# Linear attention and two MLPs: chunks 0 to 3 in 128-token tiles, the last eight chunks spread over two job slots each

## The chip, the cores and the metric

One core of a Trainium2 chip runs the whole program. The metric is device microseconds per execution; lower is better. TensorE is called PE here, its weight loads PEld, VectorE DVE, ScalarE ACT, and the queue of SyncE, from which nearly all DMAs are issued, SP.

## The reference

Attention with a decaying state (4 batches, 8 heads, 768 tokens, 64 features), then two MLPs over 3072 tokens (512 to 2048 to 512), the first gated by h times sigmoid(1.702 h), the second with a slope per feature for negative values:

```python
for t in range(S):
    state = gamma[None, :, None, None] * state + np.einsum('bhd,bhe->bhde', k[:, :, t], v[:, :, t])
    y[:, :, t] = scale * np.einsum('bhd,bhde->bhe', q[:, :, t], state)
x = np.ascontiguousarray(attn_out.transpose(0, 2, 1, 3)).reshape(B * S, H * D)
h = x @ w_in;  g = h * (1.0 / (1.0 + np.exp(-1.702 * h)));  x = g @ w_out
h = x @ w_in2; g = np.maximum(h, 0.0) + alpha * np.minimum(h, 0.0); out = g @ w_out2
```

The weights of both MLPs come in 64-bit floats.

## The kernel before

**Chunks.** The tokens are cut into 24 chunks of 128, six to a batch. A chunk needs two loads of 512 KB, qk (queries and keys by feature) and kv (keys and values by token). `att_v` (L326) scales the values by the decay on ACT, eight ops. `att_products` (L334) makes the products of a chunk in two halves of 64 tokens, each for four pairs of heads and two heads of a pair: scores `sc` (key times query), updates `pu` (key times value), and the output `px`, once from the state (`mid` in a chunk's middle, `diag` at its start) and once from the chunk's own scores `a`. That is 4 x 16 products of 64 by 64 by 64 in 32-bit floats; the trace records each as two matmuls with a weight load each. In one `att_step` (L381) the output of chunk `o` alternates with scores and updates of chunk `new`. After them DVE masks the scores (`a`, L400), adds up the state (`mid` L414, `diag` L418 and L419) and scales the output (`att_x`, L421): for chunks 0 to 7 into `x` (L427), which ACT rounds to `xhi` (L431) and DVE completes with `xlo` (L455), for later chunks into four pieces of `xl` (L446).

**The MLPs.** A block is 512 tokens. Blocks 0 and 1 (chunks 0 to 7) run through the first MLP in plain form: 32 steps, each one `mlp_h` (L538, 12 matmuls of 512 columns, `ph`) and one `mlp_y` (L554, 12 matmuls, `py`). Five steps are of block 0, 16 of block 1, and 11 of block 0 again. All the rest (`h_unit` L635, `y_chunk` L703) uses Strassen's scheme on pairs of blocks: 7 products in place of 8, in units of 6 matmuls (`pa`, `pd`) on prepared sums of inputs (`xo`, L472 and L473) and of weights (`hw`, `yw`, loaded in pieces of 256 KB). The first Strassen product is of chunks 8 to 15, the second of chunks 16 to 23.

**Order.** `job(slot, fn, ...)` books work in job slots. Slots below 0 are the launch, slots 0 to 63 lie two to a plain step (base = 64), and from 64 on there is a slot every 3.5 units. Within a slot `rank` sorts. Program order gives priorities, `tc.high_priority` raises the attention's DVE work, and a scheduler fixes each engine's order when the kernel is built. The PSUM banks are h (2), a (2) and y0 to y3; `py` holds y0 to y3 through the whole plain part.

**Chunks in slots.** Chunks 0 to 3 run in slots -10 to -2, chunks 4 to 7 in 0 to 8, chunks 8 to 15 in 36 to 52, always two slots apart, and chunks 16 to 23 in 64 to 72, one slot apart. The first `ph` of block 0 needs xhi of chunk 3, that of block 1 xhi of chunk 7. An output step of one chunk is also the scores' step of the next.

**Loads.** A ring of five 512 KB tiles (`issue`, L141) takes weights and most chunks in the order of use; a place comes free with `done`. Chunks in LOADS and chunks 1 to 3 go instead into four of the 82 SBUF slots each (`load_early`, L161). SP issues all of them in order. Weights are converted from 64-bit floats on ACT and DVE (L181 to L218), stored and loaded again as pieces; the Strassen sums of weights (L260, L283) are booked in slots 37 to 69, the Strassen inputs in 53 to 62.

**Constants.** The mask and the decays stand in `cst`; its first 76 columns are loaded first (L875).

```python
turn_at.setdefault(s, {})["new"] = c
turn_at.setdefault(s + gap, {})["o"] = c
attention(c, s - 3 if c < per else s - 1, s + gap)
```

Of the kernel before, what the change touches and what calls it, by code (L numbers as in the profile page):

```python
# [14 lines left out]
AF = mybir.ActivationFunctionType  # L15
# [4 lines left out]
P = 128  # L20
# [8 lines left out]
NLEAD = HC + H + NP  # L29
# [11 lines left out]
NQ = NF // 2  # L41
X_OF = ("b11", "b21", "t2", "t1", "t3", "b22", "t4")
# [17 lines left out]
LOADS = {5: -1, 6: 1, 7: 3}  # L60
LOADS.update({16 + n: s for n, s in enumerate((-5, -3, -1, 1, 2, 3, 4, 5))})
# [8 lines left out]
def tile_linear_attention_two_mlps(ctx: ExitStack, tc, qk, kv, w1, w2, consts, alpha, out):  # L70
# [22 lines left out]
    causal = cst[:, 0:HC]  # L93
    decay_v = cst[:, HC:HC + H]
    decay_c = cst[:, HC + H:NLEAD]
# [65 lines left out]
    def load_early(c):  # L161
        early[c] = []
        for key in (("qk", c), ("kv", c)):
            ts = []
            for n in range(2):
                ts.append(take("early"))
                nc.sync.dma_start(out=ts[n], in_=src_of(key)[:, n * 512:(n + 1) * 512])
            early[c] += ts
            loaded[key] = ts
# [154 lines left out]
    last_v = {}  # L324

    def att_v(c):  # L326
        v = take("v", (P, 2 * NP, D))
        vt = loaded["kv", c][1].rearrange("p (n d) -> p n d", d=D)
        for n in range(2 * NP):
            last = nc.scalar.activation(out=v[:, n, :], in_=vt[:, n, :], func=AF.Copy, scale=decay_v[:, n:n + 1])  # L330
        last_v[c] = last.ins
        att["v", c] = v
# [47 lines left out]

    def att_step(o, new):  # L381
        if o is not None:
            att["px", o] = att_psum(o, "px")
        if new is not None:
            att["sc", new] = att_psum(new, "sc")
            att["pu", new] = att_psum(new, "pu")
        att_products(o, new)
        if o is not None:
            give(att.pop(("v", o)), att.pop(("a", o)), att.pop(("mid", o)))
            loaded.pop(("qk", o))  # L390
            loaded.pop(("kv", o))
            if o in early:
                give(*early.pop(o))
            else:
                done()
                done()
        with tc.high_priority(HG):
            if new is not None:
                a = att["a", new] = take("a", (P, 2 * NP, HC))
                nc.vector.tensor_tensor(  # L400
                    out=a, in0=att.pop(("sc", new)).rearrange("p (n i) -> p n i", i=HC),
                    in1=causal.unsqueeze(1).to_broadcast([P, 2 * NP, HC]), op=ALU.mult,
                )
                att_state(new)
            if o is not None:
                att_x(o)
# [14 lines left out]
    def att_x(c):  # L421
        if c >= 2 * BT // C:
            att_x_kept(c)
            return
        x32 = take("x32", (P, NP, C))
        px = att.pop(("px", c)).rearrange("p (n i) -> p n i", n=NP)
        nc.vector.tensor_tensor(out=x32, in0=px, in1=decay_out, op=ALU.mult)  # L427
        j, i = divmod(c, BT // C)
        if i == 0:
            new_x(j)  # L430
        hi = nc.scalar.copy(out=x_hi[j][:, :, i * C:(i + 1) * C], in_=x32)  # L431
        if c < BT // C:
            tc.add_manual_dep(
                hi.ins, last_v[min(c + 2, BT // C - 1)].name,
                mybir.DependencyInfo(mybir.DependencyClass.NoSync, mybir.DependencyReason.DATA), reason="behind v",
            )
        att["x", c] = x32

    def att_x_kept(c):
        px = att.pop(("px", c)).rearrange("p (n i) -> p n i", n=NP)  # L440
        t, i = divmod(c % (2 * BT // C), BT // C)
        for k in range(2):
            for d in range(2):
                if i == 0:
                    xl[k, d, t] = take("xl")
                nc.vector.tensor_tensor(  # L446
                    out=xl[k, d, t][:, i * C:(i + 1) * C], in0=px[:, 2 * d + k, :],
                    in1=decay_out[:, 2 * d + k, :], op=ALU.mult,
                )
# [25 lines left out]
    def x_load(idx, t):  # L475
        assert ("x", idx) in stored
        for k in range(2):
            for d in range(2):
                xl[k, d, t] = take("xl")
                nc.sync.dma_start(out=xl[k, d, t], in_=xsd[idx][k, :, d, t])  # L480

    def x_prep(idx, n):
        which = X_OF[n]
        for k in range(2):
            sub = lambda o, x, y: nc.vector.tensor_tensor(out=o, in0=x, in1=y, op=ALU.subtract)
            if which == "t2":
                t1, t2 = xt[idx, "t1", k], xt[idx, "t2", k] = take("t1"), take("t2")
                sub(t1, xl[k, 0, 1], xl[k, 0, 0])
                sub(t2, xl[k, 1, 1], t1)
                give(xl.pop((k, 0, 0)))  # L490
            if which == "t3":
                xt[idx, "t3", k] = take("t3")
                sub(xt[idx, "t3", k], xl[k, 1, 1], xl[k, 0, 1])
                give(xl.pop((k, 0, 1)))
            if which == "t4":
                xt[idx, "t4", k] = t = xt.pop((idx, "t2", k))
                sub(t, xl[k, 1, 0], t)
                give(xl.pop((k, 1, 0)))
            if which[0] == "b":
                x_split(idx, n, k, xl[k, int(which[1]) - 1, int(which[2]) - 1])  # L500
                if which == "b22":
                    give(xl.pop((k, 1, 1)))
# [287 lines left out]
    def attention(c, s_v, s_out):  # L790
        if c in LOADS:
            job(LOADS[c] + (base if c >= 4 * per else 0), load_early, c)
            job(s_v, att_v, c)
        else:
            job(s_v, att_v, c, load=(("qk", c), ("kv", c)))
        if c < 2 * per:
            job(s_out + 1, att_x_low, c)

# [11 lines left out]
    turn_at = {}  # L810
# [54 lines left out]
    rank = [conv_hi, att_x_low, att_step, att_v]  # L865
# [92 lines left out]
def _consts():  # L958
# [4 lines left out]
    causal = np.tile(i[None, :HC] >= i[:HC, None], (2, 1))  # L963
# [3 lines left out]
    decay_v = gamma[head][:, None, :] ** -at[:, :, None]  # L967
    decay_c = gamma[head] ** C
    parts = [causal, decay_v.reshape(P, H), decay_c, decay_out.reshape(P, NP * C)]
# [44 lines left out]
```

## Time and profile before

| | |
|---|---|
| median of 3 runs | 1047.96 us (1047.56 to 1048.35) |
| the profiled execution | 1051.6 us, its span 1049.6 us |
| PE busy | 1022.6 us (97%) |
| DVE busy | 871.1 us (83%) |
| ACT busy | 679.9 us (65%) |
| DMA | 289.49 MB, mean 276 GB/s |
| chain that ended last | PE 93%, ACT 3%, DMA 1%, issue 1%, DVE 1% |
| instruction queue (q8) | 56 packets, 0.92 MB |

The span runs from the first to the last instruction. A busy PE is not PE at its peak: matmuls overlap, and their ends are modelled, so rates are better read from start to start. "issue" is time in which an engine waited for nothing that the profile shows.

### The profile page before, as it was taken

Reading aid. Unit: us, or ns where it says so; the run is one execution under the profiler, and the core shown is the slowest. Engines: PE = TensorE matmul, PEld = TensorE weight load, DVE = VectorE, ACT = ScalarE, POOL = GpSimd, SP = SyncE. Lnnn points to the kernel's source line nnn. Section 1 sums busy time; section 2 is a strip of 40 time slices with the busy share of each in tenths; the row PEclk is TensorE's granted clock in tenths of the full one; section 3 lists DMA queues with packets and bytes.
Section 4 is the critical chain, followed back from the end, with each engine's and each line's share of the span. In section 5 each row is a group of like instructions: output and inputs, shape, how many; then the busy total and the mean of one; then the engine's idle time right before and its main releaser. Section 6 shows DMA issues by size and latency. Waiting matters only on the chain.

```text
span 1049.6 us, 20177 instructions
## 1 busy us (share of the span) xinstructions
PE 1022.6 (97%) x7084; PEld 842.0 (80%) x7084; DVE 871.1 (83%) x1730; ACT 679.9 (65%) x1408; POOL 0.2 (0%) x4
## 2 busy tenths in 40 slices
PE   7889999999989999999999999999999999999998
PEld 5768888788768888888888888888888888888886
DVE  4899836898769999979799999998686987678792
ACT  5787744656766786665687686785555865556740
POOL 0000000000000000000000000000000000000000
PEclk8799999999989999999999999999999999999999
DMA  9669937899999799979989899986686676675661
GB/s 351 217 190 346 393 102 249 292 320 330 376 366 397 244 325 356 341 277 345 341 291 351 295 322 356 309 283 218 220 272 220 219 231 174 224 256 172 199 201 60
DMA packets 146405, 289.49 MB, mean 276 GB/s; under 512 B 16512, under 2 KB 16768, under 8 KB 146304
## 3 DMA queue, kind: packets, MB, share of 16 engines
q1 hardware_dynamic: 146016, 288.04, 80.1%
q8 instruction: 56, 0.92, 0.4%
q14 instruction: 45, 0.37, 0.1%
q10 hardware_dynamic: 288, 0.17, 0.1%
HBM read 213.69 MB, written 74.45 MB: 275 GB/s over the span
## 4 chain that ended last, share of the span: by engine, by line
PE 93%; ACT 3%; DMA 1%; issue 1%; DVE 1%; SPq 0%; DVEq 0%
PE py L720 36%; PE pa L647 21%; PE pd L647 16%; PE ph L545 7%; PE py L564 7%; PE px L341 3%; PE sc L341 1%; PE pu L341 1%; ACT cvr L183 1%; DMA wo<-wo 1%; ACT cvt L181 1%; PE idle L889 1%; DMA ld<-kv 0%; ACT wb L214 0%; ACT v L330 0%
## 5 line engine op out<-in xcount | busy, mean ns | idle before, releaser
L720 PE MATMUL py<-gh,yw 128*128 128x512 f32 x1120 | 299.7, 389 | 0.0
L720 PEld LDWEIGHTS py<-gh,yw 128*128 128x128 f32 x1120 | 210.2, 188 | 43.7
L647 PE MATMUL pa<-xo,hw 128*128 128x512 f32 x912 | 232.1, 391 | 0.4 <-ACT gw L516 0.4
L647 PEld LDWEIGHTS pa<-xo,hw 128*128 128x128 f32 x912 | 171.5, 188 | 37.3 <-ACT v L330 0.9
L529 DVE TENSOR_TENSOR gl<-gw,gh 128x512 fp32r<-128x512 f32 x240 | 161.4, 690 | 38.3 <-ACT gh L528 33.7
L528 ACT CAST gh<-gw 128x512 fp32r<-128x512 f32 x240 | 145.6, 620 | 56.2 <-PE py L720 26.9
L647 PE MATMUL pd<-xo,hw 128*128 128x512 f32 x684 | 176.0, 393 | 2.0 <-DVE s L260 2.0
L720 PE MATMUL py<-gl,yw 128*128 128x512 f32 x560 | 172.8, 389 | 0.0
L647 PEld LDWEIGHTS pd<-xo,hw 128*128 128x128 f32 x684 | 129.2, 189 | 29.5 <-DVE s L260 2.4
L720 PEld LDWEIGHTS py<-gl,yw 128*128 128x128 f32 x560 | 105.0, 188 | 22.1 <-DVE gl L529 0.4
L734 DVE TENSOR_TENSOR yc<-py,yc 128x512 f32<-128x512 f32 x99 | 63.8, 687 | 27.5 <-PE py L720 27.5
L521 DVE SCALAR_TENSOR_TENSOR gw<-t,nalpha,gw 128x512 f32<-128x512 f32 x96 | 71.6, 749 | 14.8 <-ACT gw L520 14.6
L519 ACT ACTIVATE t<-gw 128x512 f32<-128x512 f32 x72 | 45.5, 632 | 55.0 <-DVE gw L662 52.0
L545 PE MATMUL ph<-xhi,wb 128*128 128x512 f32 x256 | 67.4, 407 | 5.7 <-ACT xhi L431 5.5
L214 ACT CAST wb<-s 128x256 fp32r<-128x256 f32 x128 | 47.7, 402 | 31.2 <-DVE s L260 19.9
L659 ACT COPY gw<-pa 128x512 f32<-128x512 f32 x80 | 46.7, 584 | 29.5 <-PE pa L647 27.5
L564 PE MATMUL py<-gh,wb 128*128 128x512 f32 x256 | 65.4, 398 | 0.0
L545 PEld LDWEIGHTS ph<-xhi,wb 128*128 128x128 f32 x256 | 49.9, 196 | 17.3 <-ACT xhi L431 6.1
L662 DVE TENSOR_TENSOR gw<-pd,gw 128x512 f32<-128x512 f32 x80 | 55.1, 688 | 3.7 <-PE pd L647 2.9
L218 DVE TENSOR_TENSOR wb<-s,wb 128x256 fp32r<-128x256 f32 x128 | 49.8, 423 | 9.8 <-ACT wb L214 9.5
L564 PEld LDWEIGHTS py<-gh,wb 128*128 128x128 f32 x256 | 47.5, 189 | 10.5
L683 DVE TENSOR_TENSOR gw<-gw 128x512 f32<-128x512 f32 x80 | 53.9, 691 | 0.4
(90 smaller groups left out, 1366.6 us busy)
## 6 DMA issues: line engine op xcount, KB each, us to landing
hw<-wcin SPq DMA_DIRECT2D x266, 256.0 KB, 5.0
yw<-wcout SPq DMA_DIRECT2D x232, 256.0 KB, 3.8
ld<-w SPq DMA_DIRECT2D x64, 512.0 KB, 5.8
wcin<-wb SPq DMA_DIRECT2D x112, 256.0 KB, 5.1
wcout<-wb SPq DMA_DIRECT2D x88, 256.0 KB, 5.0
yw<-wo SPq DMA_DIRECT2D x48, 256.0 KB, 5.3
wo<-wb SPq DMA_DIRECT2D x32, 256.0 KB, 6.2
early<-qk SPq DMA_DIRECT2D x28, 256.0 KB, 5.8
```

What stands on the lines that cost most here:

```text
L218: nc.vector.tensor_tensor(out=w[:, 256:], in0=src, in1=w[:, 0:256].bitcast(F32), op=ALU.subtract)
L341: nc.tensor.matmul(out=ps[rows[half], cols], lhsT=lhsT, rhs=rhs, start=begin, stop=True, skip_group_check=True,)
L521: nc.vector.scalar_tensor_tensor(out=g, in0=t, scalar=nalpha[:, ft:ft + 1], in1=g, op0=ALU.mult, op1=ALU.add)
L528: nc.scalar.copy(out=gh, in_=g)
L529: nc.vector.tensor_tensor(out=gl, in0=g, in1=gh.bitcast(F32), op=ALU.subtract)
L545: nc.tensor.matmul(out=ph, lhsT=cols(w, low, k), rhs=x[:, k, :], start=(n == 0), stop=(n == len(prods) - 1),)
L564: nc.tensor.matmul(out=py[e], lhsT=lhsT, rhs=g, start=(begin and seen[e] == 1), stop=(end and seen[e] == 3))
L647: nc.tensor.matmul(out=ps, lhsT=w[:, 256 * part_ + k * P:256 * part_ + (k + 1) * P], rhs=x[2 * k + low], start=(n in (0, 1, 3) and m == 0) ...
L662: nc.vector.tensor_tensor(out=g, in0=ps, in1=g, op=ALU.add)
L683: sub = lambda o, x, y: nc.vector.tensor_tensor(out=o, in0=x, in1=y, op=ALU.subtract)
L720: nc.tensor.matmul(out=ps[e], lhsT=w[:, at:at + P], rhs=t, start=(fresh and seen[e] == 1), stop=(m == GQ - 1 and seen[e] == 3), skip_group ...
L734: add_ = lambda o, x: nc.vector.tensor_tensor(out=o, in0=ps, in1=x, op=ALU.add)
```

## The change

Chunks 0 to 3 are no longer cut into halves of 64 tokens. `launch_scores` makes their scores with all 128 keys of a pair's head against all 128 queries, into two banks, and masks them with two DVE ops; `launch_out` makes updates over 128 tokens, the output from the state and from the chunk, the new state without `mid`, and the output's scaling. Each chunk has PSUM banks of its own (`AT_LAUNCH`), and the steps of neighbouring chunks are no longer interleaved. Mask, decays and the layout of kv come in a second form for them.

Chunks 16 to 23 get a step every two slots from slot 56 on: four of them lie in the plain part (56 to 62), four in the Strassen part (64 to 70), with the last output in slot 72 as before. PSUM banks follow the slot. All chunks but 0 to 3 and 8 to 13 are loaded into SBUF slots, five job slots ahead (14 and 15 four); kv is let go after the chunk's own step, qk one step later. The tiles of `xl` are kept apart by product.

```diff
-NLEAD = HC + H + NP
+NLEAD = C + HC + 2 * H + NP
+NLAUNCH = BT // C
-LOADS = {5: -1, 6: 1, 7: 3}
-LOADS.update({16 + n: s for n, s in enumerate((-5, -3, -1, 1, 2, 3, 4, 5))})
+ATT2 = (-8, 2)
+RINGED = (8, 9, 10, 11, 12, 13)
+LEADS = ((), (5, 1), (5, 1), (4, 1), (5, 1), (5, 1))
...
+    AT_LAUNCH = (
+        {},
+        {"sc0": "y0", "sc1": "y1", "pu": "y2", "px": "y3"},
+        {"sc0": "h", "sc1": "h", "pu": "y0", "px": "y1"},
+        {"sc0": "y2", "sc1": "y3", "pu": "h", "px": "h"},
+    )
+
     def att_psum(c, which):
-        if c < BT // C:
-            tag = {"sc": "h", "pu": f"y{c % 2}", "px": f"y{2 + c % 2}"}[which]
-        elif c < 4 * BT // C:
+        if c < NLAUNCH:
+            tag = AT_LAUNCH[c].get(which, "a")
+        elif which == "sc" and turn_of[c] < base or which != "sc" and turn_of[c] + 2 < base:
             tag = {"sc": "h", "pu": "a", "px": "a"}[which]
...
+    def launch_scores(c):
+        qt, kt = loaded["qk", c]
+        att_v(c)
+        ps = [att_psum(c, f"sc{s}").rearrange("p (n i) -> p n i", n=NP) for s in range(2)]
+        for p in range(NP):
+            at = slice(p * C, (p + 1) * C)
+            for s in range(2):
+                nc.tensor.matmul(
+                    out=ps[s][:, p, :], lhsT=kt[ROWS[s], at], rhs=qt[ROWS[s], at], start=True, stop=True,
+                )
+        a = att["a", c] = []
+        for s in range(2):
+            a.append(take(f"a{s}", (P, NP, C)))
+            with tc.high_priority(HG):
+                nc.vector.tensor_tensor(
+                    out=a[s], in0=ps[s], in1=causal[C].unsqueeze(1).to_broadcast([P, NP, C]), op=ALU.mult
+                )
+
+    def launch_out(c):
...
+        for p, s, _, h in heads:
+            product(pu, s, slice(p * D, (p + 1) * D), kt[:, h * D:(h + 1) * D], v[:, h, :])
+        if c:
+            for p, s, at, h in heads:
+                product(px, 1 - s, at, diag[c % 2][ROWS[s], p, :], qt[ROWS[s], at])
+        for p, s, at, h in heads:
+            product(px, 1 - s, at, v[:, h, :], a[s][:, p, :])
...
+            if c:
+                nc.vector.tensor_tensor(out=new, in0=src, in1=diag[c % 2], op=ALU.add)
+                src = new
+            dec = decay_c.unsqueeze(2).to_broadcast([P, NP, D])
+            nc.vector.tensor_tensor(out=new, in0=src, in1=dec, op=ALU.mult)
+            att_x(c)
...
-            loaded.pop(("qk", o))
-            loaded.pop(("kv", o))
-            if o in early:
-                give(*early.pop(o))
-            else:
-                done()
-                done()
+            leave("qk", o)
+        if new is not None:
+            leave("kv", new)
...
-        hi = nc.scalar.copy(out=x_hi[j][:, :, i * C:(i + 1) * C], in_=x32)
-        if c < BT // C:
-            tc.add_manual_dep(
...
+        nc.scalar.copy(out=x_hi[j][:, :, i * C:(i + 1) * C], in_=x32)
...
     for c in range(NCH):
-        if c < per:
-            s, gap = 2 * c - 2 * per - 2, 2
-        elif c < 2 * per:
+        if c < NLAUNCH:
+            s = 2 * c - 2 * per - 1
+            job(s, launch_scores, c, load=(("qk", c), ("kv", c)))
+            job(s + 1, launch_out, c)
+            job(s + 2, att_x_low, c)
+            continue
+        if c < 2 * per:
             s, gap = 2 * (c - per), 2
+            job(s + gap + 1, att_x_low, c)
         elif c < 4 * per:
             s, gap = ATT1 + 2 * (c - 2 * per), 2
         else:
-            s, gap = base + c - 4 * per, 1
+            s, gap = base + ATT2[0] + ATT2[1] * (c - 4 * per), ATT2[1]
+        turn_of[c] = s
         turn_at.setdefault(s, {})["new"] = c
         turn_at.setdefault(s + gap, {})["o"] = c
-        attention(c, s - 3 if c < per else s - 1, s + gap)
+        if c in RINGED:
+            job(s - LEADS[c // per][1], att_v, c, load=(("qk", c), ("kv", c)))
+        else:
+            job(s - LEADS[c // per][0], load_early, c)
+            job(s - LEADS[c // per][1], att_v, c)
```

## Rows read from the trace of the kernel before

**Rows 1.** The page's head.
```profile
span 1049.6 us, 20177 instructions
```

**Rows 2.** Busy time by stage: stretch, length, busy us (x instructions) per engine, granted clock, DMA.
```profile
6.45:31.35 24.90, 15.67 (x497) 14.77 (x496) 15.12 (x33) 15.09 (x48) 0.00 (x0) 0.78 0.89 334
...
47.40:75.70 28.30, 23.67 (x378) 18.89 (x376) 27.28 (x66) 25.93 (x61) 0.00 (x0) 0.99 0.69 217
...
152.00:219.00 67.00, 65.61 (x1188) 54.36 (x1187) 51.87 (x144) 36.37 (x105) 0.00 (x0) 1.00 0.76 253
219.00:251.30 32.30, 32.30 (x145) 26.70 (x144) 30.67 (x74) 20.86 (x53) 0.00 (x0) 1.00 0.99 359
251.30:279.00 27.70, 27.70 (x499) 23.03 (x499) 21.34 (x56) 16.27 (x44) 0.00 (x0) 1.00 0.97 340
...
330.60:1049.60 719.00, 715.28 (x3155) 591.68 (x3153) 612.94 (x1085) 465.91 (x867) 0.00 (x0) 1.00 0.79 265
```

**Rows 3.** PE's waits, whole span: for whom, us in total, times, longest.
```profile
PE px L341 <- issue: 11.5, 4, 3.7
PE ph L545 <- ACT xhi L431: 5.5, 2, 4.1
...
PE pu L341 <- ACT v L330: 1.4, 1, 1.4
```

**Rows 4.** Timeline of ACT in the launch: start, us, op, [idle before <-releaser].
```profile
14.67 2.02 ACT L330 ACTIVATE v<-early,cst 128x64 f32<-128x64 f32 x8 [2.34 <-DMA early<-kv]
...
18.91 2.02 ACT L330 ACTIVATE v<-early,cst 128x64 f32<-128x64 f32 x8
...
30.68 0.62 ACT L431 CAST xhi<-x 128x512 fp32r<-128x512 f32 x1 [3.17 <-DVE x L427]
```

**Rows 5.** The launch by stretches that end at PE's stops, columns as in rows 2.
```profile
0.00:12.40 12.40, 11.19 (x221) 7.32 (x222) 4.03 (x10) 7.05 (x21) 0.20 (x4) 1.00 0.86 314
12.40:17.90 5.50, 2.99 (x128) 2.73 (x126) 3.03 (x7) 3.23 (x11) 0.00 (x0) 1.00 1.05 394
17.90:26.10 8.20, 4.66 (x126) 4.49 (x127) 5.17 (x14) 4.54 (x14) 0.00 (x0) 0.65 1.00 383
```

**Rows 6.** Timeline of PE where block 1 begins.
```profile
70.55 1.08 PE L564 MATMUL py<-gl,wb 128*128 128x512 f32 x4
75.68 3.78 PE L545 MATMUL ph<-xhi,wb 128*128 128x512 f32 x8 [4.05 <-ACT xhi L431]
...
84.10 1.98 PE L545 MATMUL ph<-xhi,wb 128*128 128x512 f32 x8
```

**Rows 7.** Stretches of small products alone and in full step, and block 1's first step.
```profile
36.77:39.06 2.29, 2.29 (x65) 2.23 (x64) 0.81 (x2) 2.18 (x6) 0.00 (x0) 0.86 0.98 354
...
159.88:161.90 2.02, 2.02 (x129) 1.95 (x129) 0.64 (x2) 1.32 (x3) 0.00 (x0) 1.00 0.00 0
...
75.70:82.00 6.30, 6.30 (x15) 4.95 (x16) 4.97 (x13) 2.43 (x5) 0.00 (x0) 0.52 0.99 259
```

**Rows 8.** DVE's groups in 251.3 to 309: count, busy us, mean ns, idle before.
```profile
L446 DVE TENSOR_TENSOR xl<-px,cst 128x128 f32<-128x128 f32 x20 | 5.2, 284 | 3.6 <-PE px L341 3.6
...
L400 DVE TENSOR_TENSOR a<-sc,cst 128x512 f32<-128x512 f32 x6 | 4.1, 686 | 3.5 <-PE sc L341 3.5
...
L414 DVE TENSOR_TENSOR mid<-pu,diag 128x256 f32<-128x256 f32 x5 | 2.1, 417 | 0.0
```

**Rows 9.** Line 647 (Strassen units) in 279.6 to 308.9: PE, PEld, clock, DMA.
```profile
279.60:308.90 29.30, 17.43 (x60) 13.02 (x61) 0.83 1.02 372
```

**Rows 10.** Chunk loads issued in 251 to 345: KB each, median us to landing.
```profile
early<-kv SPq DMA_DIRECT2D x12, 256.0 KB, 5.4
early<-qk SPq DMA_DIRECT2D x10, 256.0 KB, 5.4
```

**Rows 11.** Timeline of PE around a change to small products.
```profile
157.06 1.98 PE L545 MATMUL ph<-xhi,wb 128*128 128x512 f32 x8
158.88 1.07 PE L545 MATMUL ph<-xlo,wb 128*128 128x512 f32 x4
159.88 0.27 PE L341 MATMUL px<-ld,diag 64*64 64x64 f32 x2
```

More of the change, by code (lines that the diff above doesn't have):

```diff
@@ L92, in tile_linear_attention_two_mlps @@
     cst = cpool.tile([P, NCONST], F32, name="cst")
-    causal = cst[:, 0:HC]
-    decay_v = cst[:, HC:HC + H]
-    decay_c = cst[:, HC + H:NLEAD]
+    causal = {n: cst[:, at:at + n] for n, at in ((C, 0), (HC, C))}
+    decay_v = {n: cst[:, at:at + H] for n, at in ((C, C + HC), (HC, C + HC + H))}
+    decay_c = cst[:, C + HC + 2 * H:NLEAD]
     decay_out = cst[:, NLEAD:].rearrange("p (n i) -> p n i", n=NP)
@@ L161, in load_early @@
     def load_early(c):
-        early[c] = []
+        early[c] = {}
         for key in (("qk", c), ("kv", c)):
@@ L322, in att_psum @@
         return pool_.tile([P, 512], F32, tag=tag, name=which)
-    last_v = {}
+    ROWS = [slice(s * D, (s + 1) * D) for s in range(2)]
+    def launch_scores(c):
[15 more added lines that the diff above has]
+                )
@@ new lines, in launch_out, with product @@
+    def launch_out(c):
+        v, a = att.pop(("v", c)), att.pop(("a", c))
+        qt = loaded.pop(("qk", c))[0]
+        kt = loaded.pop(("kv", c))[0]
+        px, pu = att_psum(c, "px"), att_psum(c, "pu")
+        fresh = set()
+        def product(ps, half, cols, lhsT, rhs):
+            begin = (id(ps), half) not in fresh
+            fresh.add((id(ps), half))
+            nc.tensor.matmul(
+                out=ps[ROWS[half], cols], lhsT=lhsT, rhs=rhs, start=begin, stop=True, skip_group_check=True,
+            )
+        heads = [(p, s, slice(p * C, (p + 1) * C), 2 * p + s) for p in range(NP) for s in range(2)]
+        for p, s, _, h in heads:
[5 more added lines that the diff above has]
+            product(px, 1 - s, at, v[:, h, :], a[s][:, p, :])
+        give(v, *a)
+        if c in early:
+            give(*early[c]["qk"], *early[c]["kv"])
+        else:
+            done()
+            done()
+        att["px", c] = px
+        with tc.high_priority(HG):
+            src, new = pu[:, :NP * D].rearrange("p (n d) -> p n d", n=NP), diag[(c + 1) % 2]
+            if c:
[4 more added lines that the diff above has]
+            att_x(c)
@@ L326, in att_v @@
     def att_v(c):
         v = take("v", (P, 2 * NP, D))
+        dec = decay_v[C if c < NLAUNCH else HC]
         vt = loaded["kv", c][1].rearrange("p (n d) -> p n d", d=D)
         for n in range(2 * NP):
-            last = nc.scalar.activation(out=v[:, n, :], in_=vt[:, n, :], func=AF.Copy, scale=decay_v[:, n:n + 1])
-        last_v[c] = last.ins
+            nc.scalar.activation(out=v[:, n, :], in_=vt[:, n, :], func=AF.Copy, scale=dec[:, n:n + 1])
         att["v", c] = v
@@ L379, in att_products, with leave @@
                 f(*args, s)
+    def leave(kind, c):
+        loaded.pop((kind, c))
+        if c in early:
+            give(*early[c][kind])
+        else:
+            done()
     def att_step(o, new):
@@ L478, in x_load @@
             for d in range(2):
-                xl[k, d, t] = take("xl")
-                nc.sync.dma_start(out=xl[k, d, t], in_=xsd[idx][k, :, d, t])
+                xl[idx, k, d, t] = take("xl")
+                nc.sync.dma_start(out=xl[idx, k, d, t], in_=xsd[idx][k, :, d, t])
     def x_prep(idx, n):
@@ L788, in job @@
         jobs.setdefault(int(slot), []).append((fn, args, load))
[L790 to L797, printed above, removed]
     def convert(key, slot):
@@ L982, in by_token @@
     def by_token(a):
-        a = a.reshape(B, NP, 2, CPB, 2, HC, D).transpose(0, 3, 2, 5, 4, 1, 6)
-        return a.reshape(NCH, P, H * D)
+        whole = a.reshape(B, H, CPB, C, D).transpose(0, 2, 3, 1, 4).reshape(NCH, P, H * D)
+        a = a.reshape(B, NP, 2, CPB, 2, HC, D).transpose(0, 3, 2, 5, 4, 1, 6).reshape(NCH, P, H * D)
+        return np.concatenate([whole[:NLAUNCH], a[NLAUNCH:]])
     def weights(w_in, w_out, swap):
```

43 lines of the change are left out of this document (22 added, 21 removed).

## The prediction

> **What bounds the kernel now.** I read the page's head first [rows 1]: a span of 1049.6 us, and 1051.6 us for that execution, so 2.0 us lie around the span. The median of the runs is 1047.96 us, 3.6 below the profiled execution; I take every difference from the trace and set it off against the median. Next came the table of stages [rows 2]. The reader is to see that TensorE (PE) is the bound nearly everywhere (715 of 719 us from 330.6 on), that it is idle in three places alone, 6.45 to 31.35 (15.7 of 24.9 busy), 47.4 to 75.7 (23.7 of 28.3) and after 279, and that DVE and the DMA engines are almost full in 219 to 251.3 (30.7 of 32.3; 0.99). What follows a stage that has been shortened is therefore PE work that moves up whole. The list of PE's waits [rows 3] names them: 11.5 us for nothing that the profile shows, all at small products, and 5.5 us for xhi.
>
> **Launch: what the stops are.** Cut at PE's three stops, the launch shows 221 + 222 instructions of PE and its weight loads up to 12.4, then 128 + 126, then 126 + 127 [rows 5]: a stop every 250 or so, while DMA is at 0.86 to 1.05. The page's instruction queue brought 56 packets of 0.92 MB in all, 16 KB each. I read the stops as waits for the next piece of program, behind full DMA engines. That the cause is code is my inference; the counts are rows.
>
> **Launch: the sum.** Before, a chunk has 64 small products, each two records with a weight load each: 256 instructions. After, it has 8 scores, 8 updates, 8 from the state (none for chunk 0) and 8 from the chunk: 128. Up to chunk 3's last product that is 24 (warm) + 480 = 504 instructions against 1016, so one stop in place of three, and it falls within chunk 3, where PE waits for data anyway. What then sets the end is data: chunk 2's v waits for its DMA until 14.67, chunk 3's v begins at 18.91 and takes 2.02 [rows 4], and the loads of chunks 0 to 3 keep their order. So v ends at 20.9. Behind it come the last updates and 16 records of 128 columns. Their form is not in the trace; bounds are the 64-column stream beside nothing else, 64 records in 2.29 us or 36 ns each (0.6 us), and double that (1.2), and I add one more for the updates and take 1.7. Then x (0.69, the shape of a [rows 8]) and xhi 0.62 [rows 4], with hand-overs 1.4. The first ph comes at 20.9 + 1.7 + 1.4 = 24.0 instead of 31.35: **-7.3 us**. Bounds: 22.5 (-8.9), if products trail v closely; 29 (-2.4), if two stops of 2.5 fall behind v.
>
> Before, all launch products have one shape, 64 by 64; now K and M change three to four times a chunk. The row for a change of shape: four ph<-xlo records ahead of small products take 1.00 us (158.88 to 159.88), eight before them 1.82 or 0.23 each [rows 11], so 0.09 us for the change. Four changes on chunk 3 are 0.4 us, inside the 1.7. The Trainium skill ("TensorEngine Tiling (Array Packing)", Key Properties) says that a change of tiling mode drains the engine, which speaks against this part. By that rule all 16 changes would cost; at the row's price that is 1.4 us, with 0.4 of it behind the last data, so the sum stays; no row shows a change between two small shapes.
>
> DVE gets a second a (0.69) and loses mid (0.42) per chunk [rows 8], +1.1 us in all, on an idle engine. The first piece of constants grows from 39 to 109 KB, 0.2 us at 394 GB/s [rows 5], ahead of a v that waits for kv: nothing. Chunk 4 leaves the ring, chunks 5 to 7 load two slots earlier: each puts 1 MB, 2.7 us, ahead of weights on SP's queue, but the weights get the ring's two places; 0 to 2.7, I take 0 here, as the next term holds it.
>
> **Ramp (to 75.68).** The first ph of block 1 waits until 75.68 for chunk 7's xhi, 4.05 us after PE ran dry [rows 6]. From 47.4 DVE has 27.3 of 28.3 us busy [rows 2]. By 31.35 it had done 15.1 us of the launch stage's 24.9; done at the same share by 24.0, it is 7.3 x 0.61 = 4.5 us behind, plus 1.1: 0 to 5.6 us of the gain is lost where DVE binds. PE's steps there are near to back to back, so I lean to the low end: **+1.5 us**.
>
> **Four chunks moved in front of the Strassen part.** PE: a chunk's 128 records take 2.02 us between large products [rows 7], the same before and after the move. DVE: a 0.69, mid and the two diag 0.42 each, xl 4 x 0.28 [rows 8], 3.1 us a chunk, 12.4 for four; in 219 to 251.3 it has 1.6 us free, so some 10 us of sums and splits slide past 251.3, where 6.4 are free [rows 2] and the moved chunks' own 12.4 are gone. Cover: the sums are wanted units later. Uncovered: up to 9.2 us at the first units. SP and DMA: 16 issues of 256 KB, 10.6 us, go into stages with shares of 0.76 and 0.99. ACT: 4 x 2.0 of v, with a third free. Chunk 19's updates take y2, so they wait for the last py; behind them on PE stand the products of chunks 19 and 20 and the first Strassen units, and who waits is DVE for mid: one lone burst, 0.3 us (64 records alone 2.29, beside others 128 in 2.02 [rows 7]). The chunk tiles now sit in SBUF slots while weights still fill most of the 82; a load that waits for its slot holds SP, with stores of sums and the hw loads queued behind it. No row shows a full SBUF; 0 to 4.1 us, PE's longest wait for another engine [rows 3]; I take 0.4, as nine earlier chunks cost little. Against that the nearest row: nine such bursts in 152 to 219 cost PE one wait of 1.4 us, for v [rows 3]. I take **+1.5 us**, bounds 0.5 to 9.2.
>
> **Strassen start.** In 279.6 to 308.9 the 60 large records [rows 9] need 60 x 0.227 = 13.6 us, two whole bursts 4.0, changes 0.9: 18.5 of 29.3. So 10.8 us are lost: PE stands still, and after it a part runs at the lower of its two levels, 1.2 of 2.4 GHz (granted 0.83 as a mean). DMA is at 1.02, and each load stands in one line with the hw pieces that PE's next units need. Of that stage's loads 12 + 10 are chunk loads of 256 KB [rows 10]; six or so remain. Half the bursts, at twice the distance, 10 us of DMA less. I take 60% of the loss: **-6.5 us**, bounds -2 and -10.8.
>
> Sum: -7.3 + 1.5 + 1.5 - 6.5 = -10.8, so 1047.96 - 10.8 = **1037.2 us**.
>
> **Rivals.**
> (1) DVE eats the launch's gain in the ramp, all 5.6, and 1.7 more as weights come late: the launch nets 0, total -5.0, 1043. For: DVE's 27.3 of 28.3. Against: PE too is nearly full from 47.4 until the stop.
> (2) Slower: DVE's excess before 251.3 stands in front of PE. 9.2 lost there; the launch nets -1.7 by the same engine; the Strassen start gains 4 of 10.8, since what slides comes to lie there: +3.5, 1051.5. It decides from the point where PE waits for DVE in all over 10 us in the ramp and around 251.3. For: 1.6 us free. Against: PE waits for DVE before 251.3 hardly at all [rows 3], so its order leaves room.
> (3) Stops come with full DMA, not with the count of instructions: two stops remain behind v (-2.4), bursts stop as now (-2), the plain part pays 1.5: -2.9, 1045. For: every stop lies at a share near 1.0. Against: 250 instructions each time.
> (4) The dry 4.05 us ahead of 75.68 goes too, and with it the slow clock behind it: 0.52 granted in 75.7 to 82 [rows 7], so nearly all at 1.2 of 2.4 GHz, after PE had stood still. The step begun at 75.68 ends at 84.10, 8.42 us for 24 records that take 5.45 at 0.227 [rows 6]: 3.0 lost. -7.1 more: 1030. For: chunk 7's small products lie ahead of the py at 70.55, so PE was done with them five us before xhi; against: the priorities that order DVE's work stay.
> (5) The change doesn't do what it says: the launch ends later than its data, for the 128-column products run at a quarter of the stream's rate or ACT's v queue behind conversions (ph at 29, -2.4), and the moved chunks cost in front what they free behind: 1045.5 to 1049, no change that can be told.
>
> **How the numbers follow.** Forecast (1032 to 1041) 0.44; (1) 0.17; (2) 0.12; (3) 0.10; (4) 0.12; (5) 0.05. The range takes in (4) with a deeper Strassen gain, 1026, and ends below (2), 1047. A measurement of this kernel tells 0.2%, 2.1 us, from no change. Faster: 0.44 + 0.17 + 0.10 + 0.12 = 0.83; same 0.05; slower 0.12.
>
> **What would show it.** Launch: one stop of PE, none of the three in place; first ph near 24; the scores of chunk 3 done before its v. Ramp: first ph of block 1 near 70. Plain end: no wait of PE for DVE between 200 and 251 on the new clock, small products of chunk 19 just behind the last y. Strassen: the 30 us from the first hw unit hold some 22 us where they held 29. Wrong if ph starts past 28, if block 1's first ph hasn't moved by 4 us, or if pa or pd wait at the first units for xo or for wb.

## The result, and the profile after

| | kernel before | changed kernel |
|---|---|---|
| median, 6 runs each | 1048.1 us (1046.4 to 1051.4) | 1053.9 us (1052.6 to 1058.8) |
| ratio, 95% interval | 1 | 1.0061 (1.0036 to 1.0087) |
| profiled execution, its span | 1051.6, 1049.6 us | 1056.6, 1054.8 us |

The change makes the kernel 5.8 us slower where I forecast 10.8 us faster; my range ended at 1047. Since the gain of the launch is there, some 13 us or more were lost elsewhere. One table finds the place. I matched TensorE's large matmuls of the two traces, each kind by its order, and compared their start times:

```
matmul (us in the kernel before)        after     difference
first ph                31.35           26.86      -4.5
block 1's first ph      75.68           70.98      -4.7
a py at                195.2           188.3       -6.8
a py at                210.8           210.7       -0.2
a ph at                213.7           215.9       +2.3
first pd               254.0           272.7      +18.7   (8.4 of it: four chunks' products, moved)
a pd at                330.6           334.6       +4.0
last py               1045.5          1050.6       +5.2
```

The reader is to see three things. Launch and ramp did about what I forecast. From 195.2 to 254.0 TensorE falls back by 25.5 us; a chunk's products take some 2.1 us there [rows 7], so 8.4 us is work that was moved and **17 us is lost**, 9.1 of it by 213.7, ahead of the first moved chunk. And from there to 330.6 it gains 14.7, 6.3 beyond the 8.4.

The page's head of the changed kernel, and stages that answer to [rows 2] (columns as there):

```profile
span 1054.8 us, 19672 instructions
```
```profile
6.28:26.86 20.58, 16.50 (x231) 12.45 (x227) 15.55 (x33) 15.88 (x47) 0.00 (x0) 1.00 1.05 394
42.90:70.98 28.08, 23.25 (x378) 18.92 (x376) 26.96 (x65) 25.38 (x59) 0.00 (x0) 0.97 0.58 167
147.20:219.00 71.80, 65.42 (x1126) 53.32 (x1124) 47.78 (x131) 35.45 (x106) 0.00 (x0) 0.95 0.87 309
219.00:272.70 53.70, 49.67 (x636) 40.68 (x633) 48.22 (x123) 31.77 (x92) 0.00 (x0) 0.97 0.82 274
```

Before, TensorE was busy throughout from 219 to 279 and had 1.4 us idle from 152 to 219 [rows 2]; now it has 6.4 us idle up to 219 and 4.0 behind it, and part of both stretches runs at a lower granted clock. DVE is not what is full: 48.2 of 53.7. What TensorE waits for (against [rows 3]):

```profile
PE ph L609 <- ACT xhi L499: 5.9, 2, 4.1
PE pa L711 <- ACT gw L580: 4.5, 2, 3.5
PE px L406 <- issue: 4.1, 1, 4.1
PE px L406 <- DVE diag L486: 3.5, 3, 1.9
PE py L628 <- ACT gh L592: 1.8, 1, 1.8
...
PE pu L406 <- DVE y L642: 0.9, 1, 0.9
```

The three stops of the launch are gone; one stop "issue" of 4.1 us is new, at 206 us, and behind it the clock falls to its lower level (0.51 granted, nearly all at 1.2 of 2.4 GHz, TensorE having stood idle):

```profile
210.00:216.00 6.00, 5.74 (x19) 4.49 (x19) 3.96 (x13) 2.61 (x10) 0.00 (x0) 0.51 1.02 344
```

Just ahead of it TensorE waits 1.9 us for diag (202.2 to 204.1), and ahead of that VectorE waits, in order, for a store (until 181.5 us). VectorE's waits from 150 to 200 us, changed kernel, then the kernel before:

```profile
DVE s L262 <- DMA wcin<-wb: 5.6, 1, 5.6
```
```profile
DVE s L260 <- DMA wcin<-wb: 0.3, 1, 0.3
```

A sum tile (s) wants an SBUF slot whose last tenant (a wb) has not been written out yet. That suggests a shortage of slots. It can be counted from the code: the fewest free ones of the 82 that any take finds, by job slot.

```
job slot       42  43  44  45  46  47  48  50  52  54  56  57  58  59  60  61  62  63
before          4   5  16  15  13  11  15  21  28  34  32  29  35  29  30  29  28  24
after           4   5  12  11   5   3   9  19  24  26  19  11  18  11  17  15  19  15
```

At 44 to 49 the difference is chunks 14 and 15, which left the ring of loads (RINGED ends at 13); from 51 on it is chunks 16 to 19. The sum that waits is booked in job slot 45. There it finds 12 free slots where it found 16, and since chunk 14's four tiles have just taken the oldest, it gets the slot of a weight piece made in job slot 42, in the kernel before of one made in 38. The lowest count alone is no sign of such a wait: both kernels come down to 4 at job slot 42 and to 3 at 76, and the kernel before waits for no store at either place.

### The profile page after: what moved, and what is told of

The parts are those of the page before. It is cut to its first block, busy times and chain, and to the rows that moved or that the text cites. A ratio compares the mean times of both kernels' runs of the same rounds, so it can differ in the third digit from the quotient of the medians.

```text
span 1054.8 us, 19672 instructions
## 1 busy us (share of the span) xinstructions
PE 1025.5 (97%) x6828; PEld 841.5 (80%) x6828; DVE 870.5 (83%) x1730; ACT 675.7 (64%) x1407; POOL 0.2 (0%) x4
## 4 chain that ended last, share of the span: by engine, by line
PE 69%; DVE 14%; DMA 9%; ACT 6%; issue 2%; SPq 1%; DVEq 0%; ACTq 0%
PE py L784 30%; PE pa L711 16%; PE pd L711 11%; PE ph L609 5%; PE py L628 5%; DVE gl L593 2%; DMA wcout<-wb 2%; DVE wb L220 2%; DVE s L262 1%; DMA ld<-kv 1%; ACT v L396 1%; DVE gw L585 1%; DVE gw L726 1%; DMA wcin<-wb 1%; DMA wo<-wo 1%
## 5 line engine op out<-in xcount | busy, mean ns | idle before, releaser
L711 PE MATMUL pd<-xo,hw 128*128 128x512 f32 x684 | 173.1, 389 | 0.0
L216 ACT CAST wb<-s 128x256 fp32r<-128x256 f32 x128 | 48.2, 402 | 39.1 <-DVE s L262 25.6
L628 PE MATMUL py<-gh,wb 128*128 128x512 f32 x256 | 68.8, 413 | 1.8 <-ACT gh L592 1.8
L185 ACT ACTIVATE cvr<-ld 128x512 uint16<-128x512 uint32 x64 | 50.5, 789 | 5.5 <-DVE wsum L285 2.9
```

The source lines that it names most:

```text
L185: nc.scalar.activation(out=low, in_=w0.bitcast(U32), func=AF.Copy, scale=2.0**-29)
L216: nc.scalar.copy(out=w[:, 0:256], in_=src)
L628: nc.tensor.matmul(out=py[e], lhsT=lhsT, rhs=g, start=(begin and seen[e] == 1), stop=(end and seen[e] == 3))
L711: nc.tensor.matmul(out=ps, lhsT=w[:, 256 * part_ + k * P:256 * part_ + (k + 1) * P], rhs=x[2 * k + low], start=(n in (0, 1, 3) and m == 0) ...
```

## Theories, and the experiments

**Slots**: loads that sit in slots four or five job slots ahead make slots scarce; VectorE and SyncE's queue then wait in order for stores and releases. **VectorE**: the moved chunks' 12.4 us, or simply a full VectorE behind 195 us, take whatever TensorE gained. **Code blocks**: the "issue" stop is TensorE waiting for its program, and where it falls is a matter of position. All ratios below are to the kernel before, run on the same chip; 1 in 1000 is 1.05 us. One kernel's runs differ by some us (the kernel before: 1041.8 to 1051.4 in all), so sizes are read from the ratios, places from the traces. The difference of two ratios is uncertain by 2 to 3 us, their two intervals taken together.

### Which loads, and which place

e1_ring1415, e2_ring1619 and e3_ring1419 send chunks through the ring again (for e2: 16 to 19; for e3: 14 to 19):

```diff
-RINGED = (8, 9, 10, 11, 12, 13)
+RINGED = (8, 9, 10, 11, 12, 13, 14, 15)
```

> Chunks 14 and 15 are loaded through the ring of loads again, as before the change; the other changed chunk loads stay in job slots. Slot theory: in the changed kernel the early tiles of chunks 14 and 15 hold 8 of the 82 SBUF slots, a weight sum then waits 5.6 us on VectorE for a store to leave its slot (at 176 us), and from this come the TensorE waits between 200 and 216 us (9.1 us lost there). It expects that this wait goes, that TensorE has no gap over 1 us from 195 to 216 us, and a time of 1045 to 1047 us (1053.9 less 7 to 9). VectorE theory (the full VectorE between 200 and 260 us takes whatever TensorE gained, wherever the loads lie): 1053 to 1055, the waits of 200 to 216 us stay. Instruction-stream theory (the 4.3 us stop at 206 us has nothing to do with the slots): the stop stays, 1052 to 1054.

> Chunks 16 to 19, the four that the change moves in front of the Strassen part, are loaded through the ring instead of job slots; they stay where the change put them. Slot theory: the fewest free slots in their stretch rise from 11 to 21 or more, SyncE's wait of 5.7 us for a slot at 256 us goes, and some 4 to 8 of the 8 us lost between 216 and 272 us return: 1046 to 1050. VectorE theory (the moved chunks' VectorE work itself is too much for the stretch): 1053 to 1055, with TensorE waiting for diag, gh and gw as in the changed kernel.

> Both of the above: chunks 14 to 19 through the ring. Slot theory: the two returns add up, 1038 to 1042, about the forecast for the change. VectorE theory: 1052 to 1055. Only one of two returns: 1045 to 1050.

e4_old_places puts chunks 16 to 23 back:

```diff
-ATT2 = (-8, 2)
+ATT2 = (0, 1)
...
+LATE = dict(zip(range(16, 24), (5, 4, 3, 2, 2, 2, 2, 2)))
...
-            job(s - LEADS[c // per][0], load_early, c)
+            job(s - LATE.get(c, LEADS[c // per][0]), load_early, c)
```

> The changed kernel with chunks 16 to 23 one per job slot from the Strassen part's first slot on, as before the change, and their loads at about the old distances; launch and the slot loads of chunks 4 to 7, 14 and 15 stay changed. Slot theory: 9 us of 195 to 216 us stay lost (chunks 14 and 15 still in slots), the 8 us lost between 216 and 272 us and the 6.3 us gained at the Strassen part's start both go: 1050 to 1053. VectorE or place theory (all 17 us lost in the plain part come from the place of chunks 16 to 19): 1053.9 - 17 + 6.3, so 1042 to 1045.

Measured: e1 **1.0013** (0.9997 to 1.0030), e2 1.0052 (1.0031 to 1.0073), e3 1.0041 (1.0022 to 1.0060), e4 **1.0013** (0.9997 to 1.0030). Putting back the loads of two chunks brings 5 us, and putting back the places of the last eight, with their loads, 5 us; neither theory had it whole. In e1 VectorE's wait for the store shrinks and TensorE's wait for diag is gone (VectorE, 150 to 200 us; TensorE, 190 to 219 us), but the "issue" stop stays, which I had expected to go:

```profile
DVE s L262 <- DMA wcin<-wb: 2.5, 1, 2.5
```
```profile
PE px L406 <- issue: 3.4, 1, 3.4
```

The ring was no cure for 16 to 19, a miss of mine: the ring has five tiles, two of them are held by the partial sums until the plain part ends, and chunk 19 came late. In e3 its qk was issued at 245.5 us and landed at 252.9; TensorE, waiting, resumed at 253.0 (TensorE's waits, 190 to 262 us, put it down to a VectorE instruction that ended then):

```profile
PE sc L406 <- DVE xo L537: 5.3, 1, 5.3
```

### Slots or transfers

A chunk in slots also has four transfers on SyncE's queue where the ring has two. e13_ring1415_hold is e1 with the slots held and no load in them:

```diff
+    def hold(c):
+        held[c] = {kind: [take("hold") for _ in range(2)] for kind in ("qk", "kv")}
+        for ts in held[c].values():
+            for t in ts:
+                nc.gpsimd.memset(t[:, :8], 0.0)
...
+        if c in held:
+            give(*held[c][kind])
...
+        if c in (14, 15):
+            job(s - LEADS[c // per][0], hold, c)
```

> e1_ring1415 (chunks 14 and 15 through the ring) with the eight SBUF slots that these chunks held in the changed kernel taken and given back at the same job slots, without loads into them: only a memset of 8 columns on GpSimd in each. Slot theory: the fewest free slots fall from 13 to 5 and 11 to 3 again, a weight sum on VectorE waits several us for a store, TensorE waits about 2 us for diag near 202 us, and the 5 us that e1_ring1415 gained are lost: ratio to the kernel before 1.005 to 1.007, 1052 to 1054. Queue theory (the four loads of each chunk on SyncE's queue): as e1_ring1415, ratio 1.001, 1048 to 1049.

Measured: **1.0065** (1.0041 to 1.0089), where e1 has 1.0013 and the changed kernel 1.0061. Both waits are back (same two views as for e1):

```profile
DVE s L262 <- DMA wcin<-wb: 4.3, 1, 4.3
```
```profile
PE px L406 <- issue: 5.9, 1, 5.9
PE px L406 <- DVE diag L496: 1.6, 1, 1.6
```

So the 5 us of chunks 14 and 15 are, as near as these runs tell, the price of eight SBUF slots, and not of anything else that their loads do.

### The launch alone, and with the old launch

e5_launch_only is e4 with chunks 14 and 15 through the ring; chunks 4 to 7 stay in slots. e12_old_launch is the changed kernel with the kernel before's code for chunks 0 to 3 (halves of 64 tokens, one att_step per two job slots, the old banks):

```diff
         if c < NLAUNCH:
-            s = 2 * c - 2 * per - 1
-            job(s, launch_scores, c, load=(("qk", c), ("kv", c)))
-            job(s + 1, launch_out, c)
-            job(s + 2, att_x_low, c)
+            s, gap = 2 * c - 2 * per - 2, 2
+            turn_of[c] = s
+            turn_at.setdefault(s, {})["new"] = c
+            turn_at.setdefault(s + gap, {})["o"] = c
+            job(s - 3, att_v, c, load=(("qk", c), ("kv", c)))
+            job(s + gap + 1, att_x_low, c)
             continue
```

> The change without its second half: the new launch stays (and chunks 4 to 7 in slots), chunks 14 and 15 load through the ring as before, and chunks 16 to 23 stand one per job slot in the Strassen part as before. If the launch gain (7.6 us at 195 us in e1_ring1415) survives where nothing else is moved: 1041 to 1044. If the stretch behind 195 us takes it whatever stands there (VectorE is busy there nearly all the time): 1047 to 1049. A stop of TensorE at a code block's end (at record 195 of each 256, here near 207 and 289 us) would cost some 3 to 7 us of it: 1044 to 1047.

> The changed kernel with the old launch (chunks 0 to 3 in halves of 64 tokens); chunk loads, places and all else stay changed. If the launch is worth what launch and ramp gained (4.8 us at 75 us) wherever it ends: 1057 to 1060. If the full VectorE behind 195 us takes the launch's gain: 1053 to 1055, no difference to the changed kernel.

Measured: e5 **0.9981** (0.9967 to 0.9996), e12 **1.0120** (1.0102 to 1.0138). With the rest of the change around it the new launch is worth 6.2 us (1.0120 against 1.0061), close to my 5.8; without the rest it brings 2.0. In e5's trace (of the longest of its 12 executions, 4.0 us above their median) it leads by 7.5 us at 195.2, then a stop of 3.2 us at 203 and the slow clock behind it leave a lead of 1.9 at 213.7. The VectorE theory of e12 (no difference) falls. From e5 to e1 the new places of chunks 16 to 23 cost 3.4 us, from e1 to the changed kernel chunks 14 and 15 cost 5.

### Code blocks

Every stop named issue of 0.8 us or more from start to start, 33 in the 17 traces, lies where 193 or 194 records modulo 256 have run on TensorE (matmuls, weight loads, its sequencer's waits), and a packet of 16 KB on the instruction queue began 2.2 to 2.6 us before TensorE went on. Some of them:

```
kernel              stop, us           records ahead   packet began   from there to going on
before              297.88 to 301.81   7106 = 194      299.53         2.28
changed             205.98 to 210.26   4545 = 193      207.93         2.33
e1_ring1415         202.75 to 206.41   4546 = 194      204.00         2.41
e3_ring1419         201.20 to 203.03   4546 = 194      200.79         2.25
e4_old_places       289.36 to 294.09   6338 = 194      291.66         2.43
e13_ring1415_hold   203.29 to 209.43   4546 = 194      207.00         2.43
```

The Trainium skill ("Runtime: NRT & Kernel Launch", Instruction fetch mechanics) says that instructions come in blocks of 16 KiB, 256 of them, by a DMA queue of the engine's own, and that crossing a block is mostly hidden. The traces agree on the block, and on mostly: of some 350 block ends that lie among small products in the 17 traces about 30 show such a stop. Where it does show, it cost 0.8 to 6.1 us. What sets its length is when the packet starts: in the changed kernel the one for 205.98 began 7.0 us after the previous block's end, elsewhere in that stretch 1.0 to 4.7 us, and in the kernel before, for the same products, 1.0. Full DMA engines are not the reason in the changed kernel: from 200.9 to 207.9 they were busy 0.60 of the time. Where TensorE had waited for diag just ahead (the changed kernel, e2, e4, e12, e13) this packet began 4.4 to 8.2 us behind the block's end, elsewhere (the kernel before, e1, e3, e5, e15) 1.0 to 5.0; that the wait delays it is not shown.

e6_shift tries to move the blocks with 76 small warm-up matmuls in place of 12 large ones; e7_ring1417_shift and e8_launch_shift do the same with chunks 14 to 17 in the ring (RINGED up to 17) and on top of e5.

```diff
-WARM = 12
+WARM = 76
...
-        nc.tensor.matmul(out=idle, lhsT=warm[:, :P], rhs=warm, start=True, stop=True)
+        nc.tensor.matmul(out=idle[:D, :D], lhsT=warm[:D, :D], rhs=warm[:D, :D], start=True, stop=True)
```

> The changed kernel with 76 small warm-up matmuls on TensorE in place of 12 large ones, in about the same time: 128 more records stand ahead of everything, so TensorE's code blocks of 256 records end elsewhere. The stops that the profile names issue lie at record 194 or 195 of a block in every run so far. Code-block theory: the stop of 4.3 us at 206 us and the half clock behind it go, none over 2 us appears from 150 to 320 us, and the time is 1047 to 1050 (1053.9 less 4 to 7). VectorE theory: the stop goes, TensorE waits for VectorE instead, 1052 to 1055. If the stop has nothing to do with code blocks it stays near 206 us: 1053 to 1055.

> The changed kernel with chunks 14 to 17 loaded through the ring (18 and 19 stay in slots, since the ring has two of its five tiles held by the partial sums there and gave chunk 19 late in e3_ring1419) and with the shifted code blocks. Slots and code blocks together: the 9 us of 195 to 216 us return in full and a part of the 8 us of 216 to 272 us, 1041 to 1045. VectorE theory: 1047 to 1050.

> e5_launch_only with the shifted code blocks of e6_shift. Code-block theory: 2 to 5 us less than e5_launch_only and no stop named issue over 2 us, 1039 to 1043. Otherwise the same time as e5_launch_only.

Measured: e6 **1.0108** (1.0087 to 1.0129), e7 0.9999 (0.9983 to 1.0015), e8 0.9981 (0.9965 to 0.9998). The stop at 206 us did go, and others came at 182 us (1.0 to 2.1 us in the three), where the shifted block ends are; but the edit made the launch slower (first ph at 30.6, 29.0 and 29.4 us), so their times say little. The next edit leaves the launch alone: 64 small matmuls where TensorE stands idle for xhi, ahead of block 1.

```diff
+        if j == 1 and ft == 0:
+            for _ in range(FILL):
+                nc.tensor.matmul(out=ph[:D, :D], lhsT=warm[:D, :D], rhs=warm[:D, :D], start=True, stop=True)
+            give(warm)
```

e9_launch_fill has it on e5; e11_after_fill on the changed kernel; e14_before_fill on the kernel before; e15_launch_fill_large is e9 with 14 matmuls of 128x512 (28 records in place of 128). e10_ring1417_fill_pu has it on the changed kernel with chunks 14 to 17 through the ring and chunk 19's update off y2:

```diff
-        elif which == "sc" and turn_of[c] < base or which != "sc" and turn_of[c] + 2 < base:
+        elif turn_of[c] + 2 * (which == "px") < base:
```

> e5_launch_only with 64 small matmuls (64x64) on TensorE in front of block 1's first ph, where TensorE stands idle 4.6 us for xhi (66.6 to 71.1 us). They shift the code blocks behind them by 128 records and keep TensorE at work in the idle stretch; nothing in the launch is touched, as it was in e6_shift to e8_launch_shift (first ph there at 29 to 30.6 us where it was 26.9). Code-block theory: the stops of 3.2, 1.6 and 2.9 us at 203, 288 and 295 us go or fall below 2 us together, and the half clock behind 71 us goes: 1037 to 1042. If the stretch behind 195 us takes any gain: 1043 to 1045, as e5_launch_only. If the added matmuls delay block 1: 1045 to 1047.

> The changed kernel with the same 64 small matmuls in front of block 1 and nothing else: code blocks shifted, launch untouched, chunks 14 and 15 still in slots. Code-block theory: the stop of 4.3 us at 206 us and its half clock go, but VectorE's wait for a store (slots) and the 2.3 us that TensorE waits for diag stay: 1046 to 1050. If the slots alone set this stretch, TensorE waits for VectorE instead: 1051 to 1054.

> The changed kernel with chunks 14 to 17 through the ring, the same 64 small matmuls in front of block 1, and chunk 19's update in the bank set of the other plain chunks instead of y2 (its products waited 1.3 to 3.2 us for y2 to be read out in five runs). e7_ring1417_shift without its late launch is 2 to 3 us shorter, and the wait for y2 (3.2 us there) goes: 1039 to 1043. If the moved chunks' cost lies in VectorE's work and not in slots, code blocks and y2: 1045 to 1048.

> The kernel before with the 64 small matmuls in front of block 1's first ph (4.05 us idle there), nothing else. Code-block theory: the stops that it has now in the Strassen part (0.6, 0.8 and 3.9 us at 288, 291 and 298 us) move; by the records between them those with 128 records more in front lie near 176 and 302 us and are 1 to 2 us long, and the half clock behind 75 us goes: 3 to 5 us less, 1042 to 1044. If the matmuls gain only with the new launch: 1046 to 1047.5, no difference.

> e9_launch_fill with 14 matmuls of 128x512 in place of the 64 of 64x64: about the same time at work in the idle stretch, but the code blocks behind are shifted by 28 records in place of 128. Clock theory (what counts is that TensorE's clock does not fall at 71 us): as e9_launch_fill, ratio 0.994. Code-block theory: a stop of 1.5 to 3.8 us near 196 us and others under 2 us, ratio 0.995 to 0.998, between e9_launch_fill and e5_launch_only.

Measured: e9 **0.9940** (0.9924 to 0.9957), the best of all, 6.3 us below the kernel before; e11 1.0056 (1.0041 to 1.0071); e10 0.9969 (0.9956 to 0.9982); e14 1.0011 (0.9998 to 1.0024); e15 0.9989 (0.9972 to 1.0007).

- e9 against e15: with the blocks shifted by 128 records one stop of 1.9 us is left, with 28 there are four, 1.4 to 3.4 us, 8.3 in sum. e15 also waits 4.4 us in block 1 for y to be copied, which e9 doesn't, so the 5 us between them aren't the blocks' alone.
- e9 against e5, 4.3 us apart: over the kernel before they lead by 7.7 and 7.5 us at 195.2 and by 8.0 and 1.9 at 213.7. So what the added matmuls gain lies at e5's stop at 203 (in an execution that is a long one for e5), and not in block 1, where they run.
- e14 gains nothing, where the code-block theory had 3 to 5 us: of the three kernels that got the added matmuls alone, e5 is the one they pay on.
- The clock theory falls with the same leads of e5 and e9. e15, which was to test it, keeps TensorE as busy in the idle stretch and gains nothing on e5, but is no clean test: in e10, e14 and e15 the idle time of block 1's start came back a step later, in the first py, with a lower clock behind it (0.69 granted from 82 to 90 us in e15). TensorE's waits of e15, whole span:

```profile
PE py L634 <- ACT y L654: 4.4, 1, 4.4
PE pu L408 <- issue: 4.4, 2, 3.1
```

- e11 tells how the two causes stand to each other: no stop at 206 us is left, and yet no gain can be told (0.5 us, uncertain by 3). With slots short, TensorE comes sooner to the same waits (those of e11, 190 to 262 us):

```profile
PE px L407 <- DVE diag L487: 2.8, 3, 1.9
PE ph L614 <- ACT g L581: 1.8, 1, 1.8
PE py L633 <- ACT gh L593: 1.8, 1, 1.8
```

- e10 against e9: the moved chunks cost 3 us in time. Their traces differ by 4.1 us at 87 us already, behind e10's wait for y; from 211 to the end the difference goes from +2.8 to +3.0 us. So what is left of the moved chunks' cost, with slots and y2 dealt with, is about nothing, and not a gain.

## Why the prediction was wrong

**The failed step** is in the part on the four moved chunks: "No row shows a full SBUF; 0 to 4.1 us ...; I take 0.4, as nine earlier chunks cost little", and behind it the whole +1.5 with its bounds of 0.5 to 9.2. In place of it 17 us were lost from 195 to 254. I priced slots only for the chunks that moved and as a wait of a load; the loss began with chunks 14 and 15, which stay in place and only change from ring to slots (5 us: e1, e13), and the one who waited was VectorE, for a store. The nine earlier bursts were no evidence, since their chunks, 8 to 15, came through the ring and held no slot. What was missing is in no trace of the kernel before: the order of the code's takes and gives, by which the sum of job slot 45 now gets a slot that is still being written out. Of my signs those for launch and ramp came near the forecast; the one that failed was "no wait of PE for DVE between 200 and 251", with 3.5 us for diag, and of those that were to show me wrong none did.

**Second, the stops.** I read the launch's stops rightly as waits for the program, every 250 or so records, and then used that for the launch only. The same count applies wherever small products run. The launch lost 510 records, 2 short of two blocks, so behind it the block ends stayed at the same products; the one that stops the other kernels at 201 to 206 us cost nothing before and 4.3 us now, with the half clock behind it 6.8 (the lead falls from 4.5 us, behind the wait for diag, to -2.3 at 215.9). In e5's trace the same stop and its slow clock took 5.6 of 7.5 us.

**Launch: -7.3 forecast, -4.5 measured**, within its bounds. No stop is left (I had one). The 2.9 us have two causes. ACT: chunk 2's xhi stands ahead of chunk 3's v, which so ends at 22.9 and not 20.9 (ACT in the launch, columns as in [rows 4]):

```profile
20.32 0.62 ACT L499 CAST xhi<-x 128x512 fp32r<-128x512 f32 x1 [1.18 <-DVE x L495]
20.84 2.02 ACT L396 ACTIVATE v<-early,cst 128x64 f32<-128x64 f32 x8
...
26.18 0.62 ACT L499 CAST xhi<-x 128x512 fp32r<-128x512 f32 x1 [0.91 <-DVE x L495]
```

And the change of shape was mis-sized at 0.09 us each, four of them. pu and px products alternate in twos and fours behind v (TensorE):

```profile
21.24 0.33 PE L363 MATMUL pu<-v,early 128*64 128x64 f32 x2 [0.61 <-ACT v L396]
21.50 0.44 PE L363 MATMUL px<-early,diag 64*64 64x128 f32 x4
21.86 0.33 PE L363 MATMUL pu<-v,early 128*64 128x64 f32 x2
22.12 0.44 PE L363 MATMUL px<-early,diag 64*64 64x128 f32 x4
```

Six such records take 0.62 us from start to start. Earlier in the launch 16 pu in a row take 0.61 and 16 px 1.02, 38 and 64 ns each, so six would take 0.33: two changes cost 0.29, **0.15 us each**, and there are some eight before the last products. The trace agrees with the rule that I had cited from the Trainium skill ("TensorEngine Tiling (Array Packing)", Key Properties): a change of mode costs time. Here it cost more than the row I took.

**Ramp: +1.5 forecast**, none lost: -4.5 at the first ph, -4.7 at block 1. Rival (4) fell: the idle 4.1 us for xhi and the slow clock behind it stayed [rows 6].

**Strassen start: -6.5 forecast, -6.3 measured**, right in size and partly for the wrong reason. The 60 unit records that took 29.3 us [rows 9] take 17.6 from 297.3 on, behind a stop of 3.9 for gw (e1: 18.5). But e9 and e14, which leave the chunks there, need only 21.1 and 22.1: of the 10.8 us that I called crowding, some 7 left this stretch when the block ends lay elsewhere, among them a stop of 3.9 at 297.9 that the row for px in [rows 3] held all along. Not all of that is gained: waits for hw follow (2.7 us in e14, 3.9 in e9), and e14 as a whole is no faster. The execution that I read the 29.3 from was also 3.6 us longer than the median, so part of it may be that execution's own.

**y2**, 0.3 forecast: 0.8 to 2.9 us in the rows of eight traces with moved chunks; in e10, which avoids it, a wait of 1.0 for another bank came instead.

**Rival (2)**, slower at 1051.5, had the sign and nearly the time, not the mechanism: it was to decide where TensorE waits over 10 us for a VectorE short of time. Behind its warm-up it waits 5.1 us for VectorE (diag 3.5, y 0.9, x 0.7), and VectorE had stood idle for a store. Rival (1), the launch's gain eaten in the ramp, fell with the -4.7 at block 1. Rival (3), stops by full DMA and not by count, fell too: all lie at one count, and the launch's are gone at a DMA share of 1.05.

The parts, by ratio (us of 1047): launch, with chunks 4 to 7 in slots, -2.0; chunks 16 to 23 in their new places +3.4; chunks 14 and 15 in slots +5.0; sum +6.4. They add up by construction, as differences of neighbouring kernels (e5, e1, the changed one); taken by way of e4, chunks 14 and 15 come to 3.4 and the new places to 5.0. My terms for the same were -5.8, -5.0 and 0. Open stays which part of the moved chunks' 3.4 is y2, which slots, which block ends; and why the packet of 205.98 started so late.

## What to carry to other kernels

Before a load is moved from a ring into shared tiles, follow the pool over the whole program, take by take: how many are free, and whose tile each take gets. In a first-in-first-out pool a few more tiles held make every later take get a younger one, whose store may not be out yet, and the engine that pays is not the one that loads. Where runs of small products are long, count the instructions: each 256th is a place where the engine can stop for microseconds, and any edit ahead of it moves that place. And take the gain of a stage from what is late next in every later stage, not only in the following one.

## What the runs showed of the hardware

The packet for a code block's end starts near the end before it, in the changed kernel from some 4 us ahead of that to 8.2 us behind it, and at the 33 stops TensorE goes on 2.2 to 2.6 us after the start. A whole block of small products and their weight loads runs in 2.0 us [rows 7]; so unless the packet starts early, it takes large matmuls or an idle stretch within the block to cover it.

What TensorE does before its first real products sets their pace, and the granted clock's column doesn't tell. After 12 matmuls of 128x512 (1.2 to 5.5 us) the 16 px of chunk 0 take 1.03 us, 64 ns each; after 76 of 64x64 in the same time they take 1.90, 119 ns each, and the pace comes back only at 16.6 us. Both stretches read 1.00 (changed kernel, then e6_shift; columns as in [rows 2]):

```profile
10.00:12.00 2.00, 2.00 (x40) 1.64 (x38) 1.35 (x3) 1.75 (x7) 0.00 (x0) 1.00 1.04 388
```
```profile
10.00:12.00 2.00, 2.00 (x16) 1.75 (x16) 0.42 (x1) 1.13 (x5) 0.00 (x0) 1.00 1.07 394
```

For e6 that 1.00 is no reading: its trace lists no granted level before 16.50 us, where the list begins with the full clock, and a stretch without an entry reads 1.00. In the changed kernel the list begins at 4.25 us, in e7 and e8 at 12.7 and 13.9. A little over half the pace up to that moment is near what the lower of the two levels would give. This cost e6 3.7 us at the first ph.
